# Fused attention and gated MLP: the rows of block 0 taken straight from the score tile, softmax ahead of the conversion in four steps, one score unit fewer in step 0

## The chip, the cores and the metric

The kernel runs on one core of a Trainium2 chip. The core has five engines that matter here: TensorE (PE) with its matrix product and, beside it, the loading of weights (PEld); VectorE (DVE); ScalarE (ACT); GpSimd (POOL); and SyncE (SP), which in this kernel does nothing but issue DMA transfers. Data lies in DRAM, in SBUF (128 partitions, the place of the tiles) and in PSUM (the banks into which PE writes).

The metric is the device time of one execution in microseconds (us), as the median of several runs. A profiled execution has its own time, and in it a span, from the first to the last recorded instruction.

## The reference, cut to what matters

```python
# q, k, v: (8, 12, 448, 64); w_pre, w_post: (12, 12); fp32 throughout
scores = np.matmul(q, k.transpose(0, 1, 3, 2)) / np.sqrt(64)
scores = np.einsum('bhij,hg->bgij', scores, w_pre)         # mix over the heads
scores = scores - np.max(scores, axis=-1, keepdims=True)
attn = np.exp(scores)
attn = attn / (np.sum(attn, axis=-1, keepdims=True) + 1e-09)
attn = np.einsum('bhij,hg->bgij', attn, w_post)            # mix over the heads
out = np.matmul(attn, v)
x = out.transpose(0, 2, 1, 3).reshape(3584, 768)
a, b = x @ w1, x @ w2                                      # (768, 1024) each
y = ((a * b) @ w3) @ w_out                                 # (1024, 1024), (1024, 768)
```

The part of the program that the change touches computes the scores of batch element 0, mixes them over the heads and takes the softmax of the first rows.

## The kernel before, in words

**Rows and blocks.** After the scores come the two mixes over heads. For these the kernel needs a tile in which one partition holds one row of one head. It takes 10 query rows (IB) of 12 heads (H) at a time: 120 partitions (GI) with 448 elements each, a *row block*. A batch element has 45 of them (NB; the last ones overlap or are short), and the main loop runs over all row blocks of all batch elements, one a step.

**From scores to rows.** PE computes the scores of a head for 112 query rows at a time (JT; four such chunks make the 448): partition = query row. A row block wants partition = (query row, head). The turn is made through DRAM: the scores of batch element b are stored to `raw_d[b]`, with the shape [448 rows, 12 heads, 448 columns], and `fetch(n)` (line 217) loads row block n from there into the tile `r`, one transfer of 120 rows of 1,792 bytes. Three buffers hold `r` tiles in turn.

**Batch element 0 at the start.** Queries and keys arrive for two heads (a *pair*, six of them) in the tiles `kqz0` to `kqz5`: a first part (the first 112 query columns and all keys) and a second part (the other query columns, line 867, `others(p)`). `qk_first(p, c, banks)` computes chunk c of pair p; its two matrix products (line 158, tile `psz`) are copied out of PSUM by DVE and, for the second head, by DVE or ACT (lines 163 and 164). For chunk 0 the copies go into one SBUF tile that holds the 112 rows of all 12 heads, `sz`; they are stored to DRAM in two parts. The first FIRST = 48 rows are stored pair by pair (line 168, six stores of 48 rows of 3,584 bytes):

```python
        if c == 0:
            dst, st = dst[:FIRST], st[:FIRST]
        return lambda: nc.sync.dma_start(dst, st)
```

The remaining 64 rows go for all pairs at once, 21,504 bytes a row, when the loads of the first row blocks are already issued (line 800, below the "big store"):

```python
        held = lambda: nc.sync.dma_start(self.raw_d[0][FIRST:JT], self.sz[FIRST:])
```

The other three chunks of the six pairs are 18 *score units*, handed out over the steps 0 to 14 (`firsts`, line 803); one such unit is called ahead of the conversion of the step and any others behind it. A unit needs the second part of its pair's `kqz`.

**A step of the main loop** (`for n in range(N + 6)`) issues, in program order: the load of row block n + 4 (`fetch`), stores that were put off (`do_later`), a second part of `kqz` (`others(n + 3)`), then work on the engines: conversion pieces, `softmax(n)`, `scale(n - 1)`, a split of rows for a later step (`split_r`), score units, the second mix of an earlier block (`post`) and the first mix of the next one, `mix(n + 1)`. The first mix is a product on PE with a block-diagonal `w_pre` (line 235 in the first 20 row blocks, `psm<-r,wsc`). The softmax is a minimum on DVE (`mn`), and the exponential with its running sum on ACT (line 249, `e`, `sm`).

**Conversion.** Beside that, the weights of the MLP arrive as words (`cs`, line 96: `cs3<-wo` is a 128 x 768 piece of w_out's words), go through a square on ACT (line 102, `cm<-cs`), four operations on DVE and a split into a high and a low part (a cast on ACT at line 121, and POOL). `converting()` is a generator, and each `next(...)` makes one piece; the pieces feed `folding`, the product of w3 and w_out.

**What sets the order.** On every engine the instructions run in the order in which the program is written. All DMA transfers go through SP's queue, one behind the other; a store or load that has to wait for data (or for a semaphore of an earlier transfer) holds up those behind it. So the order of SP around the big store is that of these lines:

```python
        others(0)
        others(1)
        for n in range(LF - 1):     # LF = 4
            self.fetch(n)
        next(fold_pieces)
        next(fold_pieces)
        held()
```

Tiles named below: `kqz` (queries and keys of a pair), `psz` and `sz` (scores in PSUM and SBUF), `r` (row block), `wpre_s` and `wsc` (the block-diagonal matrix of the first mix, as loaded and scaled), `psm` (mixed scores), `mn`, `e`, `sm` (minimum, exponential, sum), `cs`, `cm`, `cx`, `fw`, `fo` (conversion and its results).

Of the kernel before, what the change touches and what calls it, by code (L numbers as in the profile page):

```python
# [6 lines left out]
F32 = mybir.dt.float32  # L7
# [8 lines left out]
B, H, S, D = 8, 12, 448, 64  # L16
DM, FF = 768, 1024
HP = H // 2
IB = 10
GI = H * IB  # L20
NB = -(-S // IB)
JT, NJ = 112, 4
# [1 line left out]
NG = NB // GB  # L24
KF, K1 = FF // 128, DM // 128
WHOLE = 20
FIRST = 48
CW = 384
DH = DM // 2
LATE = 2 * NB + GB + 2  # L30
# [15 lines left out]
class Kernel:  # L46
# [102 lines left out]
    def qk_first(self, p, c, banks):  # L149


        nc, t = self.nc, self.kq0s[p]
        cols = slice(c * JT, (c + 1) * JT)
        q = slice(S + cols.start, S + cols.stop) if c else slice(0, JT)
        ps = [self.bank(i, f"psz{p}_{c}_{s}")[:JT, :S] for s, i in enumerate(banks)]
        for s in range(2):
            rows = slice(s * D, (s + 1) * D)
            nc.tensor.matmul(ps[s], t[rows, q], t[rows, JT:JT + S], start=True, stop=True)
        if c == 0:
            st = self.sz[:, 2 * p:2 * p + 2]  # L160
        else:
            st = (self.qp if p % 2 else self.kp).tile([JT, 2, S], F32, tag="st", name=f"sz{p}_{c}", bufs=2)
        nc.scalar.copy(st[:, 0], ps[0])
        (nc.scalar.copy if c else nc.vector.tensor_copy)(st[:, 1], ps[1])
        dst = self.raw_d[0][cols, 2 * p:2 * p + 2, :]
        if c == 0:
            dst, st = dst[:FIRST], st[:FIRST]
        return lambda: nc.sync.dma_start(dst, st)

    def load_kq(self, b, p):  # L170
# [571 lines left out]
    def run(self):  # L742
        nc, tc = self.nc, self.tc
# [29 lines left out]
            nc.sync.dma_start(self.kq0s[p][:, :JT + S], self.kq0[p][:, :JT + S])  # L773
        self.sz = self.mp.tile([JT, NJ, H, GB * IB], F32, tag="mt", name="sz")
        self.sz = self.sz.rearrange("p j g i -> p (j g i)")[:, :H * S].rearrange("p (h j) -> p h j", h=H)
        w = self.kp.tile([128, S], F32R, tag="qh", name="wpre_s").bitcast(F32)[:GI, :GI]
        self.wsc = cp.tile([GI, GI], F32, name="wsc")
        nc.sync.dma_start(w, self.wpre)
# [8 lines left out]
        self.wph = cp.tile([GI, GI], F32R, name="wph")  # L787
        self.wpl = cp.tile([GI, GI], F32R, name="wpl")
        held = []
        for p in range(HP):  # L790
            held.append(self.qk_first(p, 0, ((0, 1), (2, 3), (6, 7))[p % 3]))
            if p > 1:
                held.pop(0)()
        nc.vector.tensor_copy(self.wph, self.wsc)
        nc.vector.tensor_tensor(self.wpl, self.wsc, self.wph.bitcast(F32), op=ALU.subtract)
# [2 lines left out]
        for f in held:  # L798
            f()
        held = lambda: nc.sync.dma_start(self.raw_d[0][FIRST:JT], self.sz[FIRST:])  # L800
        firsts = {}
        for u in range(HP, HP * NJ):
            firsts.setdefault((u - HP) * 15 // (HP * NJ - HP), []).append((u % HP, u // HP))

# [1 line left out]
        for b in range(1, B):  # L808
            first, per, ahead = (12, 26 / 48, 2) if b == 1 else ((b - 1) * NB - 6, 45 / 48, 3)
            for u in range(H * NJ):  # L810
                h, c = divmod(u, NJ)
                n = first + int(u * per)
# [10 lines left out]
        N = B * NB  # L823
# [29 lines left out]
        def advance(count):  # L853
            nonlocal done
            for _ in range(min(count, total - done)):
                next(background)
                done += 1

        def there(p):

            f, r = divmod(p - 3 - 2 * KF, 3)
            return 2 * KF * 3 * (1 + f) + (0, 9, 18)[r] if f >= 0 else min(max(3 * (p - 3), 0), KF * 3)

        wanted, LF, turn = 0, 4, itertools.chain((6, 7, 0) * 9, itertools.cycle((6, 7)))
        self.v_list = [(b, a, g) for b in range(B) for a in range(NG) for g in range(HP)]
        def others(p):
            nc.sync.dma_start(self.kq0s[p][:, JT + S:], self.kq0[p][:, JT + S:])

        others(0)
        others(1)  # L870
        for n in range(LF - 1):
            self.fetch(n)
        next(fold_pieces)
        next(fold_pieces)
# [15 lines left out]
        for n in range(N + 6):  # L890
            self.step = n
            if n == GB + 1:
                self.close("qp")
                self.xp = [self.pool("xp0", 1)]
            if n == SWITCH:
                assert done == total
                next(background, None)
                self.do_ends()
                self.do_soon()
                self.do_later()  # L900
                assert not fold_pieces
                self.close("fp")
                self.wp = self.pool("wp", 5, side="right")
                self.up = self.pool("up", 1, side="right")
                self.xp.append(self.pool("xp1", 1, side="right"))
                background, total, done = self.experts(phases), (E_1 + E_2) * ONE + P_1 * (B - ONE) // 2, 0
            if n == LATE:
                assert done >= E_1
                self.close("xp0", "cx")
                self.xq, self.cb = self.pool("xq", 2), self.pool("cb", 1)  # L910
            if n == PAIR:

                assert done >= 2 * E_1 + E_2 and unit_pieces is None and not self.jobs and not self.ys
                self.do_ends()
                self.do_soon()
                self.do_later()
                self.pairs, self.w_ahead = True, 4
                self.close("xp1", "cb", "xq", "cs")
                self.xq = self.pool("xq", 2)
                self.up2 = self.pool("up2", 1, side="right")  # L920
                self.free += range(N_UP, NS)
                setup = self.pair_setup(phases)
            if PAIR <= n < PAIR + 7:
                next(setup, None)
            if LF <= n + LF < N:
                self.fetch(n + LF)
            self.do_later()
            if n + 3 < HP:
                others(n + 3)
            elif 2 * HP - 3 <= n < 2 * HP:  # L930
                self.load_v()
            for x in loads.get(n, []):
                self.load_kq(*x)
            for x in splits.get(n, []):
                self.split_kq(*x, nc.gpsimd, nc.gpsimd)

            p, pieces = self.n_made - 1 if fold_pieces else 2 * KF + 3 * KF, None
            if avs.get(n):
                pass
            elif fold_pieces:  # L940
                f = (self.n_made - 1 - 2 * KF) // 3
                if f < 2 or done >= 2 * KF * 3 * (f - 1):
                    pieces = fold_pieces
                    if next(pieces, self) is self:
                        fold_pieces = pieces = None
            if n < N:
                self.softmax(n)
            if 0 <= n - 1 < N:
                self.scale(n - 1)
            if n + 2 < N:  # L950
                self.split_r(n + 2)
            self.do_soon()
            for x in firsts.get(n, [])[:1]:
                self.later.append(self.qk_first(*x, (next(turn), next(turn))))
            for x in qks.get(n, []):
                store = self.qk(*x, nq % 2, nc.scalar.copy)
                nq += 1
                if store:
                    self.later.append(store)
            if pieces:  # L960
                next(pieces)
            elif unit_pieces and not fold_pieces and not avs.get(n):
                ahead = 1 if n < SWITCH else 2 * done // (3 * K1) + 4 + (done > 0)
                if n_pieces < ahead:
                    n_pieces += 1
                    if next(unit_pieces, self) is self:
                        unit_pieces = None
                    else:
                        next(unit_pieces)
            now = share.get(n, 0)  # L970
            if n < SWITCH:

                wanted += now
                now = max(min(there(p), KF * 3 + wanted) - done, 0)
            self.do_sums()

            advance(now // 2)
            if 0 <= n - 2 < N:
                self.post(n - 2)
            for x in firsts.get(n, [])[1:]:  # L980
                self.later.append(self.qk_first(*x, (next(turn), next(turn))))
            for x in avs.get(n, []):
                self.av(*x)
            advance(now - now // 2)
            if n + 1 < N:
                self.mix(n + 1)
            self.do_ends()
# [68 lines left out]
```

## Time and profile before

| | |
|---|---|
| Median of 3 runs | 1639.13 us (1638.95 to 1643.07) |
| Profiled execution | 1639.43 us, span 1637.7 us |
| Mean granted clock of PE | 0.993 |
| PE busy | 1579.9 us, 96% of the span |
| PEld, DVE, ACT, POOL busy | 86%, 63%, 61%, 65% of the span |
| DMA | 446.10 MB in 233,906 packets, mean 272 GB/s |

How to read the rows that follow. A group of instructions is given as line, engine, operation and its tiles as out<-in, with the shapes and the count (x). In a timeline the first two columns are start and duration in us from the start of the span, and a bracket tells the idle time ahead of the instruction and what ended it. "SPq" is SP's queue of DMA issues: the duration there is the time that the issue took on the queue, with whatever it waited for, not the transfer. The DMA view gives for each kind of transfer the count, the size and the median time from issue to landing, and for a window the packets by size and their rate. The granted clock of PE is given as a share of full speed. Tile names leave out the buffer number, so `kqz` is any of the six and `r` any row block.

### The profile page before, as it was taken

To read this page: it belongs to the slowest core of one execution; us is meant where nothing else is said; L and a number is where in the kernel's file an instruction comes from. 1 tells how busy PE (TensorE), PEld (TensorE's weight loads), DVE (VectorE), ACT (ScalarE), POOL (GpSimd) and SP (SyncE) were. 2 spreads that over 40 slices of the span, in tenths; PEclk is the share of its full clock that TensorE was granted. 3 is DMA by queue.
4 is the path that set the end of the run, shared out by engine and by line. 5 is a ranking of instruction groups with operands and counts; after the bars stand their busy time and mean duration, and the time that the engine had idled before them with its cause. 6 is when DMAs were issued, how large, how long until landed. Compare 5 with 4: busy or idle time off the path is not lost. (4 is left out here: it accounts for less than half of the span.)

```text
span 1637.7 us, 31687 instructions
## 1 busy us (share of the span) xinstructions
PE 1579.9 (96%) x10528; PEld 1414.0 (86%) x10528; DVE 1030.6 (63%) x2302; ACT 997.3 (61%) x2413; POOL 1068.5 (65%) x902
## 2 busy tenths in 40 slices
PE   5999999999999999999999999999999999999999
PEld 2578997887898888889899898899999898999988
DVE  5967768778747767863465565745555557634573
ACT  4877657677666776776666666666765554542321
POOL 1346546667657788885576776876675666655774
PEclk7999999999999999999999999999999999999999
DMA  8988879898899999999978977889978756678875
GB/s 263 342 269 275 255 223 302 277 310 288 264 279 310 321 341 315 323 335 306 312 240 279 290 243 238 257 270 309 305 248 250 238 188 196 211 229 302 281 233 179
DMA packets 233906, 446.10 MB, mean 272 GB/s; under 512 B 21838, under 2 KB 159054, under 8 KB 233678
## 3 DMA queue, kind: packets, MB, share of 16 engines
q1 hardware_dynamic: 233742, 444.08, 84.6%
q8 instruction: 83, 1.36, 0.4%
q14 instruction: 81, 0.66, 0.1%
HBM read 309.90 MB, written 134.09 MB: 271 GB/s over the span
## 5 line engine op out<-in xcount | busy, mean ns | idle before, releaser
L227 POOL TENSOR_TENSOR rl<-r,rh 120x448 fp32r<-120x448 f32 (+1 forms) x340 | 425.0, 1250 | 321.9 <-DVE rh L226 108.0
L246 DVE TENSOR_REDUCE mn<-psm 120x1 f32<-120x448 f32 x360 | 223.8, 622 | 410.1 <-PE psm L240 395.1
L249 ACT ACTIVATE e<-psm,mn 120x448 f32<-120x448 f32 x360 | 228.5, 635 | 348.1 <-DVE sa L258 293.4
L272 PEld LDWEIGHTS pso<-w,e 120*112 120x112 f32 (+1 forms) x2880 | 345.5, 177 | 49.4 <-ACT mt L278 35.0
L272 PE MATMUL pso<-w,e 120*112 120x120 f32 (+1 forms) x2880 | 358.9, 267 | 20.6 <-ACT mt L278 20.2
L703 PE MATMUL e<-eh,wu 128*128 128x448 f32 x1008 | 304.4, 371 | 1.1 <-DVE c L657 1.1
L278 ACT COPY mt<-pso 112x480 f32<-112x480 f32 x360 | 206.9, 575 | 14.9 <-PE pso L272 9.9
L703 PEld LDWEIGHTS e<-eh,wu 128*128 128x128 f32 x1008 | 187.3, 188 | 16.1 <-DVE c L657 1.9
L226 DVE CAST rh<-r 120x448 fp32r<-120x448 f32 (+1 forms) x340 | 189.9, 559 | 4.1 <-DMA r<-raw_d 3.0
L703 PE MATMUL e<-el,wu 128*128 128x448 f32 x504 | 187.6, 372 | 2.4 <-POOL el L642 2.4
L198 ACT COPY st<-psq 112x448 f32<-112x448 f32 x336 | 173.3, 527 | 25.8 <-DMA raw_d<-st 25.7
L303 PE MATMUL psa<-mt,v 112*64 112x150 f32 (+1 forms) x2304 | 156.9, 292 | 1.9 <-DMA v<-v 1.9
L183 POOL TENSOR_TENSOR ql<-kq,qh 128x448 fp32r<-128x448 f32 x84 | 99.2, 1181 | 85.1 <-ACT qh L181 84.9
L303 PEld LDWEIGHTS psa<-mt,v 112*64 112x64 f32 x2304 | 143.6, 137 | 8.1 <-DMA v<-v 2.3
L657 DVE TENSOR_TENSOR c<-c,e 128x448 f32<-128x448 f32 x168 | 101.2, 615 | 70.4 <-PE e L703 65.8
L193 PE MATMUL psq<-kk,qh 128*112 128x448 f32 x336 | 125.7, 374 | 8.0 <-ACT st L198 7.8
L238 PE MATMUL psm<-rh,wph 120*120 120x448 f32 (+1 forms) x340 | 129.6, 381 | 0.0
L523 PE MATMUL eg<-xh,wu 128*128 128x448 f32 x384 | 127.3, 381 | 0.0
L240 PE MATMUL psm<-rl,wph 120*120 120x448 f32 (+1 forms) x340 | 124.1, 365 | 0.6 <-POOL rl L227 0.5
L239 PE MATMUL psm<-rh,wpl 120*120 120x448 f32 (+1 forms) x340 | 124.2, 365 | 0.0
L194 PE MATMUL psq<-kk,ql 128*112 128x448 f32 x336 | 122.8, 365 | 0.0
L642 POOL TENSOR_TENSOR el<-x,eh 128x448 fp32r<-128x448 f32 x90 | 105.7, 1195 | 9.3 <-DMA x<-x_d 5.3
(114 smaller groups left out, 2961.7 us busy)
## 6 DMA issues: line engine op xcount, KB each, us to landing
r<-raw_d SPq DMA_DIRECT2D x352, 210.0 KB, 4.1
raw_d<-st SPq DMA_DIRECT2D x168, 392.0 KB, 4.7
wu<-w_d SPq DMA_DIRECT2D x104, 384.0 KB, 5.6
wu<-s_d SPq DMA_DIRECT2D x96, 384.0 KB, 4.4
v<-v SPq DMA_DIRECT2D x144, 224.0 KB, 5.1
kq<-kq SPq DMA_DIRECT2D x42, 672.0 KB, 7.0
wu<-w_d SPq DMA_DIRECT2D x51, 512.0 KB, 5.9
wu<-s_d SPq DMA_DIRECT2D x36, 512.0 KB, 4.4
```

Of the source, the lines that this page charges most:

```text
L193: nc.tensor.matmul(p, qh[:, cols], kk, start=True, stop=False)
L198: copy(st[:, c % 2], p)
L226: nc.vector.tensor_copy(rh[:K], r[:K])
L227: nc.gpsimd.tensor_tensor(rl[:K], r[:K], rh[:K].bitcast(F32), op=ALU.subtract)
L238: nc.tensor.matmul(p[:K, :S], self.wph[:K, :K], rh[:K], start=True, stop=False)
L246: nc.vector.tensor_reduce(mn[:K], p[:K, :S], axis=AX.X, op=ALU.min)
L249: nc.scalar.activation(e[:K], p[:K, :S], AF.Exp, bias=mn[:K], scale=-1.0, accum_out=sm[:K])
L272: nc.tensor.matmul(p[:, j, :, :w], e[:K, j * JT:(j + 1) * JT], w2[:K, :, :w], start=True, stop=True)
L278: self.ends.append((4, lambda: copy(dst, p[:, :, :, :w])))
L303: nc.tensor.matmul(self.psa[rows, g % 3, :W], v[:, j, rows], mt[:, j, 2 * g + s, :W], start=(j == 0), stop=(j == NJ - 1))
L523: nc.tensor.matmul(p, u[:, k % (K1 // 2), x], xs[y][:, k], start=(k == 0 and t == 0), stop=(k == K1 - 1 and t == 2))
L703: nc.tensor.matmul(p, w[:, k, x], ops[m, k][y], start=(k == 0 and t == 0), stop=(k == nk - 1 and t == 2))
```

## The change

It has four parts.

1. **Row block 0 from SBUF.** In chunk 0, `qk_first` now copies the first 10 rows of each head straight from the score tile into the tile `r` of row block 0, every twelfth partition of it: 12 copies of 10 rows of 1,792 bytes, those of the even heads issued by ACT and those of the odd heads by SP. The load of row block 0 from DRAM goes. The pairs' row stores leave these 10 rows out. FIRST becomes 50, so a row store has 40 rows instead of 48, and the big store 62 instead of 64. A pair's copies are issued when its scores are computed; its row store is put off for three pairs instead of two.
2. **kqz0's second part** is issued right behind the six first parts, ahead of `wpre`, instead of behind the row stores.
3. **Softmax ahead of the conversion** in the steps 0 to 3.
4. **Score units**: one in step 0 instead of two, and the other 17 spread over the steps from 1 on.

```diff
-FIRST = 48
+FIRST = 5 * IB
...
         if c == 0:
-            dst, st = dst[:FIRST], st[:FIRST]
+
+            for h in range(2 * p, 2 * p + 2):
+                (nc.sync if h % 2 else nc.scalar).dma_start(self.rs[0][h::H], self.sz[:IB, h])
+            dst, st = dst[IB:FIRST], st[IB:FIRST]
         return lambda: nc.sync.dma_start(dst, st)
...
             nc.sync.dma_start(self.kq0s[p][:, :JT + S], self.kq0[p][:, :JT + S])
         self.sz = self.mp.tile([JT, NJ, H, GB * IB], F32, tag="mt", name="sz")
...
+        nc.sync.dma_start(self.kq0s[0][:, JT + S:], self.kq0[0][:, JT + S:])
         w = self.kp.tile([128, S], F32R, tag="qh", name="wpre_s").bitcast(F32)[:GI, :GI]
         self.wsc = cp.tile([GI, GI], F32, name="wsc")
         nc.sync.dma_start(w, self.wpre)
...
         held = []
+        self.rs[0] = self.rp.tile([GI, S], F32, tag="r", name="r0", bufs=3)
         for p in range(HP):
             held.append(self.qk_first(p, 0, ((0, 1), (2, 3), (6, 7))[p % 3]))
-            if p > 1:
+            if p > 2:
                 held.pop(0)()
...
         held = lambda: nc.sync.dma_start(self.raw_d[0][FIRST:JT], self.sz[FIRST:])
         firsts = {}
         for u in range(HP, HP * NJ):
-            firsts.setdefault((u - HP) * 15 // (HP * NJ - HP), []).append((u % HP, u // HP))
+            firsts.setdefault((u - HP - 1) * 14 // (HP * NJ - HP - 1) + 1, []).append((u % HP, u // HP))
...
-        others(0)
         others(1)
-        for n in range(LF - 1):
+        for n in range(1, LF - 1):
             self.fetch(n)
         next(fold_pieces)
         next(fold_pieces)
...
             for x in splits.get(n, []):
                 self.split_kq(*x, nc.gpsimd, nc.gpsimd)
+            if n < 4:
+                self.softmax(n)
 
             p, pieces = self.n_made - 1 if fold_pieces else 2 * KF + 3 * KF, None
...
-            if n < N:
+            if 4 <= n < N:
                 self.softmax(n)
             if 0 <= n - 1 < N:
                 self.scale(n - 1)
```

The order of the instructions on the engines that the change moves, before and after. (The lines of the code shift by three to five, so that the big store is L800 before and L805 after.)

SP (its DMA issues) in the start, from the words `cs1` of w3 on to the second part of pair 1, before. The row stores of line 168 write the first rows of the score tile `sz` to `raw_d`:

```order
L96 DMA cs1_145<-w3t 128x3x256
L168 DMA raw0_d_62<-sz_136 48x896 x4
L96 DMA cs2_192<-w3t 128x2x256
L168 DMA raw0_d_62<-sz_136 48x896 x2
L867 DMA kqz0_124<-kq0 128x336
L867 DMA kqz1_125<-kq0 128x336
```

And after (six of the twelve copies are here, the other six on ACT):

```order
L96 DMA cs1_146<-w3t 128x3x256
L169 DMA r0_151<-sz_136 10x448 x4
L171 DMA raw0_d_62<-sz_136 40x896
L169 DMA r0_151<-sz_136 10x448
L171 DMA raw0_d_62<-sz_136 40x896
L169 DMA r0_151<-sz_136 10x448
L171 DMA raw0_d_62<-sz_136 40x896
L96 DMA cs2_205<-w3t 128x2x256
L171 DMA raw0_d_62<-sz_136 40x896 x3
L872 DMA kqz1_125<-kq0 128x336
```

The copies into `r0` come ahead of and between the row stores, which move behind them, and kqz0's second part has left this place.

SP right behind that, around the big store, before:

```order
L217 DMA r0_206<-raw0_d_62 120x448
L217 DMA r1_208<-raw0_d_62 120x448
L217 DMA r2_210<-raw0_d_62 120x448
L96 DMA cs3_212<-wo 128x768
L800 DMA raw0_d_62<-sz_136 64x5376
L96 DMA cs4_226<-wo 128x768
L217 DMA r3_240<-raw0_d_62 120x448
L867 DMA kqz2_126<-kq0 128x336
L217 DMA r4_243<-raw0_d_62 120x448
```

And after:

```order
L220 DMA r1_219<-raw0_d_62 120x448
L220 DMA r2_221<-raw0_d_62 120x448
L96 DMA cs3_223<-wo 128x768
L805 DMA raw0_d_62<-sz_136 62x5376
L96 DMA cs4_237<-wo 128x768
L220 DMA r3_251<-raw0_d_62 120x448
L872 DMA kqz2_126<-kq0 128x336
L220 DMA r4_254<-raw0_d_62 120x448
```

The load of r0 is gone, the big store has 62 rows, and what stands ahead of and behind it is otherwise the same: kqz2 is the third transfer behind it.

PE from the first mix on (row block 0), before:

```order
L235 MATMUL psm0_238<-r0_206,wsc_138 120x448
L158 MATMUL psz0_1_0_257<-kqz0_124 112x448
L158 MATMUL psz0_1_1_258<-kqz0_124 112x448
L158 MATMUL psz1_1_0_270<-kqz1_125 112x448
L158 MATMUL psz1_1_1_271<-kqz1_125 112x448
L235 MATMUL psm1_277<-r1_208,wsc_138 120x448
L158 MATMUL psz2_1_0_301<-kqz2_126 112x448
L158 MATMUL psz2_1_1_302<-kqz2_126 112x448
L235 MATMUL psm2_314<-r2_210,wsc_138 120x448
```

And after:

```order
L238 MATMUL psm0_249<-r0_151,wsc_139 120x448
L158 MATMUL psz0_1_0_268<-kqz0_124 112x448
L158 MATMUL psz0_1_1_269<-kqz0_124 112x448
L238 MATMUL psm1_281<-r1_219,wsc_139 120x448
L158 MATMUL psz1_1_0_304<-kqz1_125 112x448
L158 MATMUL psz1_1_1_305<-kqz1_125 112x448
L158 MATMUL psz2_1_0_317<-kqz2_126 112x448
L158 MATMUL psz2_1_1_318<-kqz2_126 112x448
L238 MATMUL psm2_324<-r2_221,wsc_139 120x448
```

The mix of row block 1 moves ahead of the score unit of pair 1; the unit of pair 2, which needs kqz2, keeps its place ahead of the mix of block 2.

ACT in the first two steps, before:

```order
L121 CAST fw0_214<-cx2_236 128x2x128
L102 ACTIVATE cm3_250<-cs3_212 128x384
L249 ACTIVATE e0_254,sm0_255<-psm0_238,mn0_252 120x448
L163 COPY sz0_1_261<-psz0_1_0_257 112x448
L164 COPY sz0_1_261<-psz0_1_1_258 112x448
L163 COPY sz1_1_274<-psz1_1_0_270 112x448
L164 COPY sz1_1_274<-psz1_1_1_271 112x448
```

And after:

```order
L252 ACTIVATE e0_259,sm0_260<-psm0_249,mn0_257 120x448
L121 CAST fw0_225<-cx2_247 128x2x128
L102 ACTIVATE cm3_266<-cs3_223 128x384
L163 COPY sz0_1_272<-psz0_1_0_268 112x448
L164 COPY sz0_1_272<-psz0_1_1_269 112x448
L252 ACTIVATE e1_289,sm1_290<-psm1_281,mn1_287 120x448
L121 CAST fo_143<-cx3_279 128x384
L102 ACTIVATE cm4_296<-cs4_237 128x384
L163 COPY sz1_1_308<-psz1_1_0_304 112x448
```

The exponential of block 0 moves ahead of the cast and of the square that wants cs3, and pair 1's copy out of PSUM moves behind the exponential of block 1 and the square that wants cs4. On DVE and POOL the order is the same before and after.

## The prediction

> **What bounds the kernel now.** I read the page first (parts 1 and 2), then the busy times by stage, cut where the picture of TensorE (PE) changes (after each engine's busy time its instructions; the last three columns are the granted clock, the DMA engines' busy share and what they moved), then PE's own timeline in the start, and from its last wait back to SyncE's (SP's) transfers.
>
> ```profile
> core 0: us, PE busy (x) PEld busy (x) DVE busy (x) ACT busy (x) POOL busy (x), PEclk, DMA share, GB/s
> 20.00:32.00 12.00, 6.97 (x14) 2.10 (x14) 5.57 (x12) 4.79 (x12) 1.72 (x2) 0.64 0.89 264
> 32.00:38.00 6.00, 6.00 (x16) 2.06 (x17) 2.97 (x9) 3.23 (x8) 1.00 (x1) 0.57 0.94 303
> 38.00:64.00 26.00, 25.82 (x131) 15.03 (x130) 23.33 (x52) 20.11 (x48) 6.02 (x6) 1.00 0.99 338
> 64.00:100.00 36.00, 30.81 (x136) 17.55 (x136) 28.54 (x69) 31.06 (x76) 17.16 (x16) 0.91 0.97 332
> 100.00:1637.60 1537.60, 1502.11 (x10218) 1373.67 (x10214) 960.01 (x2143) 931.22 (x2262) 1040.41 (x871) 1.00 0.85 270
> ```
>
> From 100 us on PE is busy 1502.1 of 1537.6 us at full clock, and from 38 to 64 us 25.8 of 26. What the change moves lies ahead of that. So whatever it does to the moment at which PE runs without a stop goes into the end almost one to one; only the stage from 64 to 100 us, in which PE stands 5.2 us, could take some of it up.
>
> PE's timeline of the start (start, duration, line, tiles; in brackets the idle time before and what ended it):
>
> ```profile
> 20.18 1.82 PE L235 MATMUL psm<-r,wsc 120*120 120x448 f32 x2 [8.21 <-DMA r<-raw_d]
> 21.93 2.54 PE L158 MATMUL psz<-kqz 64*112 64x448 f32 x6
> 25.78 1.00 PE L158 MATMUL psz<-kqz 64*112 64x448 f32 x2 [1.31 <-ACT sz L163]
> 26.71 1.64 PE L235 MATMUL psm<-r,wsc 120*120 120x448 f32 x2
> 31.89 1.84 PE L158 MATMUL psz<-kqz 64*112 64x448 f32 x4 [3.54 <-DMA kqz<-kq]
> 33.66 1.85 PE L235 MATMUL psm<-r,wsc 120*120 120x448 f32 x2
> 35.44 1.84 PE L158 MATMUL psz<-kqz 64*112 64x448 f32 x4
> ```
>
> The change is aimed at the first wait, 8.21 us for the rows r0. But the last wait decides: at 31.89 PE has stood 3.54 us for the second part of pair 2's queries (kqz2, line 867), and from there on it runs. Everything ahead of 31.89 may move by some us and PE still waits for kqz2. So I follow kqz2. SP's timeline; below it the time from issue to landing (last column) of single transfers, from the DMA view of windows around one issue: the issues at 19.15 and 18.75, then those at 19.85 and 22.68, and r0's at 17.39:
>
> ```profile
> 17.39 1.25 SPq L217 DMA_DIRECT2D r<-raw_d  x3
> 18.75 0.36 SPq L96 DMA_DIRECT2D cs<-wo  x1
> 19.15 0.61 SPq L800 DMA_DIRECT2D raw_d<-sz  x1
> 19.85 0.53 SPq L96 DMA_DIRECT2D cs<-wo  x1
> 20.43 2.21 SPq L217 DMA_DIRECT2D r<-raw_d  x1
> 22.68 2.52 SPq L867 DMA_DIRECT2D kqz<-kq  x1
> 29.31 0.35 SPq L217 DMA_DIRECT2D r<-raw_d  x1
> ```
>
> ```profile
> raw_d<-sz SPq DMA_DIRECT2D x1, 1344.0 KB, 10.1
> cs<-wo SPq DMA_DIRECT2D x1, 384.0 KB, 5.3
> ...
> cs<-wo SPq DMA_DIRECT2D x1, 384.0 KB, 10.5
> ...
> kqz<-kq SPq DMA_DIRECT2D x1, 168.0 KB, 9.1
> ...
> r<-raw_d SPq DMA_DIRECT2D x1, 210.0 KB, 2.6
> ```
>
> The big store of line 800 (the rest of the score tile, 64 rows of 21,504 bytes) is issued at 19.15 and lands 10.1 us later, at 29.25. cs4 and kqz2, issued behind it, land behind it, at 30.3 and 31.8, though a transfer of kqz2's size is soon done: r0, which is larger, took 2.6 us in an emptier queue. So kqz2 is late because it stands behind the big store, and the question is what the change does to that store: its FIRST goes from 48 to 50, and the store from 64 rows to 62.
>
> **How many DMA engines a transfer uses.** The small packets tell: the DMA queue over the whole span, then from 19.0 to 19.5 us, then in two windows of 0.02 us (packets, MB, share of 16 engines).
>
> ```profile
> DMA packets 233906, 446.10 MB, mean 272 GB/s; under 512 B 21838, under 2 KB 159054, under 8 KB 233678
> ...
> r<-raw_d SPq DMA_DIRECT2D x352, 210.0 KB, 4.1
> ...
> wpre_s<-wpre SPq DMA_DIRECT2D x1, 56.2 KB, 4.7
> ```
>
> ```profile
> DMA packets 112, 0.17 MB, mean 348 GB/s; under 512 B 15, under 2 KB 112, under 8 KB 112
> ```
>
> ```profile
> q1 hardware_dynamic: 1, 0.02, 249.7%
> ...
> q1 hardware_dynamic: 1, 0.02, 533.1%
> ```
>
> The whole list of issues adds up to 1372 transfers. Of the 21,838 packets under 512 bytes, 240 are the rows of wpre and of wpo, its like (120 of 480 bytes each). 21,598 remain. With one closing packet from each of 16 engines they would be 21,952; 354 are missing, exactly as many as there are transfers of 120 rows (352 + 2). So a transfer of 120 rows runs on 15 engines, 8 rows each, and those of 128, 112, 96, 64 and 48 rows on 16. The second fence shows it once: from 19.0 to 19.5 us, when r0 finishes, 15 small packets. Rows dealt out one by one would have used 16 engines for 120 rows; groups of eight would have used 6 for 48. Two readings are left. (A) Equal shares: the largest number up to 16 that divides the rows. (B) Rows over 16, rounded up, for each engine until none is left. They agree on every count of this trace and part at 62: by A 2 engines with 31 rows, by B 16 with up to 4. I take A, since no transfer in the trace has an unequal share. The Trainium skill's page "DMA: Bandwidth & Descriptors" (section "Why a DMA increments its semaphore by 16 and not by 1") says that a transfer issued on SP or ACT takes the largest k up to 16 that divides the slowest dimension of both sides. By that rule the sum is the one below, by B about 1639; the trace agrees with it at 120 rows, and no run here shows 62.
>
> The price of a row: in each of the two short windows, at 23.68 and 22.82 us, one packet of the big store starts. 2.497 x 16 x 0.02 = 0.80 us; the other took 1.71 us. I take 0.80, which is 27 GB/s; the stage from 38 to 64 us moved 338/16 = 21 GB/s per engine, beside many others, so 1.02 us is the slow end.
>
> **The change part by part.**
> - The big store, by A: 31 x 0.80 = 24.8 us. When does it start? Ahead of it SP now issues six copies into r0 (the other six go from ACT), and one load less. At 1.25/3 = 0.42 us each that is at most +2.1 us, and at least 0 if SP's waits for landings hide them; I take +1.0, so 20.2. r0's 2.6 us less 0.5 for its data make 2 us from issue to the first packet, and r1, r2, cs3 ahead of it about 0.5: start 22.7, end 47.5. Ends: 22.2 and, if it waits for all of cs3 (18.75 + 5.3 + 1), 25.1.
> - kqz2 behind it: today 31.8 - 29.25 = 2.5 us later. It keeps its share on each engine, the store's two among them, so it lands at 50.0 instead of 31.8: **+18.2 us**. PE stands in that time. Late next are cs4 and r3, which land just ahead of kqz2.
> - r4 no longer waits for the store's landing (SP stands today from 25.2 to 29.3): 0, for it lands behind the store anyway. r5 still waits for it.
> - r0 straight from the score tile: mix(0) some 3 us earlier, at best; cost or gain 0 while kqz2 decides. The six issues on ACT, at 0.42 each, lie ahead of 20 us where PE stands: 0, at most 2.5 us, which also lies ahead of 31.89. Row stores of 40 rows: by A 10 engines with 4 rows instead of 16 with 3: 0 for the same reason.
> - kqz0's second part ahead of wpre: 168 KB at the 264 to 338 GB/s of the stages delay wpre and wsc by 0.5 to 0.7 us. PE needs wsc at 20 us only: 0.
> - Softmax ahead of the conversion: today ACT's exp of row block 0 stands behind the square that waits for cs3:
>
> ```profile
> 24.14 0.55 ACT L102 ACTIVATE cm<-cs 128x384 f32<-128x384 f32 x1 [3.91 <-DMA cs<-wo]
> 24.60 0.61 ACT L249 ACTIVATE e<-psm,mn 120x448 f32<-120x448 f32 x1
> ```
>
>   Now it stands ahead of it, up to 3.9 us earlier, inside PE's wait: 0. In return pair 1's score copies come behind the square of cs4, which lands just before kqz2, and pair 2 needs a bank that they free: 0 to +0.9 us. I take 0.
> - One score unit in step 0: 1.84 us of PE move behind mix(1), both ahead of 31.89: 0.
>
> Sum: the profiled execution took 1639.43 us (span 1637.7), 0.3 over the median of the runs, 1639.13. On the median: 1639.1 + 18.2 = **1657.3 us**. Ends: start 22.2 gives +17.7; start 25.1 at 1.02 us a row gives 25.1 + 31.6 + 2.5 = 59.2, +27.4. Two unknowns reach below: the stage from 64 to 100 us may give back some of its 5.2 us, and the clock (0.57 to 0.64 here) may come back sooner or later by a us or two. So the likeliest case has 1651 to 1666.
>
> **The rivals.**
> - B, not slower: 62 rows still spread over 16 engines. Then kqz2 moves with SP's order alone: 0 to +2.1 us for the issues, less some 0.6 us for 205 KB that need not be moved (a load of 210 KB, 168 KB of row stores and 42 of the big store go, 215 KB of copies come, at 330 GB/s): -0.6 to +1.5 us, and a step of the clock either way. 1636.5 to 1642, most likely 1639. It decides where the store's landing stays within 12 us of its issue. For it speaks that the store has always been fast; against it the missing packets, which show that the count of rows matters.
> - C, worse: on its two engines each row takes the 1.71 us of the other row shown. 53.0 us, kqz2 at 78: +46, 1685. Against it: long packets mostly lie where several transfers are in flight on one engine.
> - That the change does not do what it says: r0 is complete only after its last copy, which stands behind row stores on SP; mix(0) might start no earlier than 20 us. Under A and B alike that changes nothing at 31.89, so it has no time of its own.
>
> **How the numbers follow.** A 0.86, B 0.10, C 0.04. The prediction is A's 1657.3. For 8 in 10 I take 1649 to 1666, nearly all of A; the rest is B, C and A's edges. 0.3% is 4.9 us, about what a measurement of this kernel can tell from no change. All of A and C is slower by more: 0.90. B is within it but for a small part: same 0.09, faster 0.01.
>
> **What would show it.** After: the big store lands some 27 us after its issue, not 10; a wait of PE for kqz2 of over 20 us that ends near 50; ten small packets, not 16, for each copy into r0 and each row store; DMA share near 2/16 in between, and from 52 us on the old picture, shifted. mix(0) earlier than 20 us. Wrong, if the store lands within 12 us: then it is B, and the time is that of today.

## The result and the profile after

The changed kernel takes 1669.11 us (median of 4 runs, 1668.45 to 1669.17) against 1639.04 us: 1.0179 times as long, 95% interval 1.016 to 1.0197 (here and below the ratio is estimated from the runs of both kernels and isn't the quotient of the two medians; they differ by up to 0.2%). By the medians that is 30.1 us more, where 18.2 were forecast; the range ended at 1666. The direction and the main mechanism were right, the size was not. The profiled execution took 1669.17 us, its span is 1667.4 us.

The busy times by stage, with each stage from 62 us on laid 30 us behind its like of before:

```profile
core 0: us, PE busy (x) PEld busy (x) DVE busy (x) ACT busy (x) POOL busy (x), PEclk, DMA share, GB/s
20.00:32.00 12.00, 6.66 (x10) 1.36 (x6) 5.85 (x14) 3.83 (x10) 1.72 (x2) 0.64 0.75 233
32.00:62.00 30.00, 0.00 (x0) 0.00 (x0) 0.04 (x1) 0.56 (x3) 0.99 (x1) 0.50 0.13 42
62.00:94.00 32.00, 30.85 (x135) 16.16 (x136) 26.65 (x59) 23.78 (x56) 7.04 (x7) 0.89 0.95 304
94.00:130.00 36.00, 30.45 (x130) 17.47 (x129) 28.20 (x66) 30.64 (x73) 16.84 (x16) 0.91 1.00 332
130.00:1667.40 1537.40, 1505.71 (x10231) 1376.65 (x10230) 963.50 (x2148) 931.21 (x2264) 1039.89 (x872) 1.00 0.85 271
```

Everything that was added is the second row: 30 us in which the engines do next to nothing (ACT 0.56 us, POOL 0.99) and the DMA engines are busy for a share of 0.13, which is 2 of 16. From 130 us on the rows are those of before from 100 us on (PE 1505.7 busy us of 1537.4, against 1502.1 of 1537.6 before). PE's timeline names both ends of the hole, SP's what stands in it:

```profile
17.77 1.82 PE L238 MATMUL psm<-r,wsc 120*120 120x448 f32 x2 [3.34 <-DMA r<-sz]
...
25.82 1.85 PE L238 MATMUL psm<-r,wsc 120*120 120x448 f32 x2 [4.60 <-DMA r<-raw_d]
27.60 3.66 PE L158 MATMUL psz<-kqz 64*112 64x448 f32 x4
62.98 1.89 PE L158 MATMUL psz<-kqz 64*112 64x448 f32 x4 [31.71 <-ACT sz L163]
```

```profile
14.20 0.74 SPq L169 DMA_DIRECT2D r<-sz  x1
...
17.44 1.17 SPq L171 DMA_DIRECT2D raw_d<-sz  x3
18.66 0.70 SPq L872 DMA_DIRECT2D kqz<-kq  x1
23.04 0.77 SPq L220 DMA_DIRECT2D r<-raw_d  x2
24.31 0.28 SPq L805 DMA_DIRECT2D raw_d<-sz  x1
24.69 0.36 SPq L96 DMA_DIRECT2D cs<-wo  x1
...
60.84 0.34 SPq L220 DMA_DIRECT2D r<-raw_d  x1
```

The hole begins at about 31.3, where the matmuls of 27.60 end. The first mix starts at 17.77 instead of 20.18 us: the rows of block 0 do come earlier. But the last row stores are issued up to 18.6 us instead of 14.2, r1 and r2 wait on SP until they have landed (23.04), and the big store of 62 rows goes out at 24.31 instead of 19.15. It lands at about 60.8, when SP may issue r5, which needs its rows. cs4 and kqz2, issued behind it, land behind it.

PE's bracket names ACT (pair 1's copy out of PSUM, line 163; lines 163 and 164 are ACT's, but for the second head of a pair in chunk 0, which is DVE's), because that copy now stands behind the square that wants cs4:

```profile
62.01 0.55 ACT L102 ACTIVATE cm<-cs 128x384 f32<-128x384 f32 x1 [29.46 <-DMA cs<-wo]
62.46 0.52 ACT L163 COPY sz<-psz 112x448 f32<-112x448 f32 x1
```

ACT itself waited 29.46 us for cs4. This is the same transfer jam seen one step later, and the order on ACT adds at most a microsecond to it.

The number of engines can be counted again. In the whole span:

```profile
DMA packets 233911, 445.89 MB, mean 267 GB/s; under 512 B 21893, under 2 KB 159109, under 8 KB 233685
```

There are 1383 transfers now. 16 closing packets each would be 22,128. Take off one for each of 353 transfers of 120 rows, 6 for each of the 12 copies (10 rows) and the 6 row stores (40 rows), and 14 for the big store, if it runs on 2 engines: 21,653 remain. With the 240 rows of wpre and wpo that is 21,893, the number counted. ACT's queue shows it for its six copies alone:

```profile
q10 hardware_dynamic: 120, 0.11, 0.0%
```

That is 60 rows and 60 more packets, 10 for each copy of 10 rows.

How fast did the two engines go? Two windows in the hole, at first and then later (packets, MB, rate):

```profile
DMA packets 18, 0.39 MB, mean 55 GB/s; under 512 B 0, under 2 KB 0, under 8 KB 0
```

```profile
DMA packets 26, 0.56 MB, mean 33 GB/s; under 512 B 0, under 2 KB 0, under 8 KB 0
```

From 33 to 40 us 18 rows start, 7 x 2 / 18 = 0.78 us of an engine a row, as forecast. From 41 to 58 us it is 17 x 2 / 26 = 1.31 us, though nothing else is in flight (the windows hold no smaller packets).

### The profile page after: what moved, and what is told of

The parts are those of the page before. It is cut to its first block, busy times and chain, and to the rows that moved or that the text cites. A ratio compares the mean times of both kernels' runs of the same rounds, so it can differ in the third digit from the quotient of the medians.

```text
span 1667.4 us, 31715 instructions
## 1 busy us (share of the span) xinstructions
PE 1585.2 (95%) x10528; PEld 1416.3 (85%) x10528; DVE 1032.4 (62%) x2302; ACT 996.0 (60%) x2413; POOL 1067.7 (64%) x902
## 2 busy tenths in 40 slices
DMA packets 233911, 445.89 MB, mean 267 GB/s; under 512 B 21893, under 2 KB 159109, under 8 KB 233685
```

## The experiments

Each is compared with runs of the kernel before on the same chip, so its ratio counts, not the difference to 1639.04. The time of a single profiled execution can lie some us off the median of its kernel. "Before" and "changed" below are the two kernels.

**1. The changed kernel with its big store in 48 + 14 rows.**

```diff
-held = lambda: nc.sync.dma_start(self.raw_d[0][FIRST:JT], self.sz[FIRST:])
+def held():
+    nc.sync.dma_start(self.raw_d[0][FIRST:98], self.sz[FIRST:98])
+    nc.sync.dma_start(self.raw_d[0][98:JT], self.sz[98:])
```

> The changed kernel with its big store cut in two, rows 50 to 97 (48 rows) and rows 98 to 111 (14 rows). Theory 1 (the number of rows sets the number of engines: 62 = 2 x 31 gives 2, 48 gives 16, 14 gives 14): the store is done some 10 us after its issue again. Its issue stays at 24.3 us instead of 19.15, so PE's last wait of the start ends near 37 instead of 31.9 and the time is +5 us or less over before: 1640 to 1645 us. Theory 2 (it is the first partition, 50 instead of 48, that makes the store slow): the 48 rows still begin at partition 50, so the time stays near 1669. Theory 3 (it is the copies into r0 and the late row stores that cost): also near 1669.

Measured 1644.71 us against 1637.67, ratio 1.0031 (1.0017 to 1.0045). PE's last wait ends at 38.04:

```profile
38.04 1.84 PE L158 MATMUL psz<-kqz 64*112 64x448 f32 x4 [7.27 <-ACT sz L163]
```

The same rows from the same partitions, cut in two, take some 24 us off 1669.1. Theories 2 and 3 fall as explanations of the bulk; some 5 us remain.

**2. The kernel before with its big store in 62 + 2 rows** (the same edit with the cut at 110).

> The kernel before, all of it, but its big store of 64 rows cut into 62 rows (48 to 109) and 2 rows. Theory 1: 62 rows run on 2 engines; issued at 19.15, first row at 21.7, 31 rows an engine at the 1.05 us a row that the changed kernel's trace averages gives a landing near 55 and kqz2 near 57.5 instead of 31.8: +25 us, 1664 (at 0.80 us a row, 1657). Theory 2 (first partition) and theory 3 (copies and late row stores): nothing of theirs is in it, 1639.

Measured 1663.64 us against 1637.67, ratio 1.0145 (1.0126 to 1.0165). PE's wait and SP's issue of the row block that needs the store:

```profile
57.76 1.84 PE L158 MATMUL psz<-kqz 64*112 64x448 f32 x4 [30.04 <-DMA kqz<-kq]
```

```profile
19.72 0.28 SPq L801 DMA_DIRECT2D raw_d<-sz  x1
...
53.61 0.32 SPq L217 DMA_DIRECT2D r<-raw_d  x1
```

Two rows fewer in one transfer (they go as a store of their own), and nothing else of the change, cost 26 us. Here PE's bracket names kqz2, as the prediction had it.

**3. The kernel before with its big store in 61 + 3 rows** (the cut at 109).

> The kernel before with its big store cut into 61 rows (48 to 108) and 3 rows. Theory 1: 61 is prime, so one engine takes all rows: 61 x 0.80 to 1.10 us = 49 to 67 us after 21.7, landing at 71 to 89, time 1679 to 1697 us. If instead anything not a multiple of 16 falls back to two engines: as with 62 rows, 1657 to 1664. If the rows are dealt out, 1639.

Measured 1681.36 us against 1637.67, ratio 1.0248 (1.0229 to 1.0268). The store is issued at 19.11 and lands at 72.1. The window from 40 to 70 us:

```profile
DMA packets 37, 0.80 MB, mean 27 GB/s; under 512 B 0, under 2 KB 0, under 8 KB 0
q1 hardware_dynamic: 37, 0.80, 6.2%
```

6.2% is one engine of 16. It needs 30 / 37 = 0.81 us a row, and it doesn't slow down. So fewer rows take longer: the divisor of their number counts, not the amount.

**4. The changed kernel with the stores of before**: FIRST is 48 again and a row store has all 48 rows.

```diff
-FIRST = 5 * IB
+FIRST = 48
-            dst, st = dst[IB:FIRST], st[IB:FIRST]
+            dst, st = dst[:FIRST], st[:FIRST]
```

> The changed kernel with FIRST at 48 and row stores of all 48 rows (the 10 rows that r0 has got directly are stored too), so both kinds of stores have the sizes of before, and the rest of the change stays. Theory 1: the big store takes 10 us again; issued 3 to 5 us later than before because the row stores are, the time is 1639 to 1644. Theory 3: stays near 1669. The difference to the run with 48 + 14 rows shows what row stores of 40 instead of 48 rows cost (10 engines with 4 rows each, against 16 with 3): 0 to 2 us.

Measured 1643.26 us against 1637.67, ratio 1.0028 (1.0015 to 1.0041). SP issues the big store at 24.26, and PE's last wait ends at 36.84:

```profile
24.26 0.59 SPq L805 DMA_DIRECT2D raw_d<-sz  x1
```

```profile
36.84 1.84 PE L158 MATMUL psz<-kqz 64*112 64x448 f32 x4 [5.18 <-ACT sz L164]
```

Row stores of 40 instead of 48 rows make no difference that the intervals of runs 1 and 4 would show (the two also differ in the big store, 48 + 14 rows against 64). What remains of the change still costs 0.3%, and its PE starts 5 us late.

**5. The kernel before with its big store in 16 + 34 + 14 rows**, to see why two engines slow down.

> The kernel before with its big store cut into 16, 34 and 14 rows (48 to 63, 64 to 97, 98 to 111); 34 = 2 x 17, so the middle piece runs on 2 engines by the count of rows. It is to tell why the rows of the 2-engine stores took 0.80 us each at first and 1.3 us later. Theory H (where the two engines read): the slow part begins when both read partitions from 64 on; here both do so from the first row (64 to 80 and 81 to 97), so rows take about 1.3 us from the start, some 22 us for 17. Theory G (a matter of how far the transfer has come, or of the partitions from 96 on): 17 rows at 0.80 us, some 13.6 us, with two slow ones at most. Time: the store lands 15 to 24 us after its first row instead of 7: 1643 to 1655 us.

One run, 1650.02 us. From about 30 to 36.6 us nearly all rows of the 34-row store take 0.80 us on both engines. Only its last three, the 17th of one engine and the 16th and 17th of the other, take 1.2 to 1.4 us, and the row of the next store behind them on each of these engines 1.95 and 0.91. Theory H falls: if the shares are consecutive rows, both engines read from partition 64 on all the time.

**6. The kernel before with the rest of the change, without the copies**: kqz0 early, softmax ahead, one score unit in step 0; r0 comes from DRAM and the stores are those of before. The edits are the parts 2 to 4 of the change.

> The kernel before with everything of the change but the copies into r0, their held-back row stores and FIRST: kqz0's second part ahead of wpre, softmax ahead of the conversion in steps 0 to 3, one score unit in step 0. Theory C (the 5 us that the changed kernel loses even with stores on 16 engines come from the copies, whose issues on ACT and SP make the row stores and with them r1 and the big store late): the big store is issued near 19 us again, PE's last wait ends near 32, time 1636 to 1640 us. Rival D (they come from the early load or the new order on ACT and PE): PE's last wait ends near 37 and the time is 1641 to 1645 us.

Measured 1637.45 us against 1638.84, ratio 0.9985 (0.9974 to 0.9996).

```profile
20.40 0.61 SPq L801 DMA_DIRECT2D raw_d<-sz  x1
```

```profile
32.32 1.84 PE L158 MATMUL psz<-kqz 64*112 64x448 f32 x4 [3.81 <-DMA kqz<-kq]
```

Without the copies the loss is gone, as theory C of the expectation has it; these three parts may even gain a little. This is the only version whose interval lies below the kernel before. The big store still goes out at 20.40 instead of 19.15, so not all of its delay is the copies'.

**7. Run 4 with the row stores held back for two pairs** (`p > 1`).

> The changed kernel with stores of 48 and 64 rows as in the run before (FIRST 48, whole row stores), and a pair's row store held back for two pairs instead of three, as in the kernel before. If holding them back is what makes the big store late, its issue goes from 24.3 back to 20 to 21 us and the time to 1638 to 1640 us. If the copies' own issues do (0.73 us each on ACT, between the copies of the scores out of PSUM, and as much on SP), it stays at 23 to 25 us and the time at 1641 to 1645 us.

Measured 1644.18 us against 1638.84, ratio 1.0023 (1.001 to 1.0037). SP's timeline:

```profile
16.44 0.74 SPq L169 DMA_DIRECT2D r<-sz  x1
17.28 0.41 SPq L171 DMA_DIRECT2D raw_d<-sz  x1
18.26 1.36 SPq L171 DMA_DIRECT2D raw_d<-sz  x2
...
24.14 0.59 SPq L805 DMA_DIRECT2D raw_d<-sz  x1
```

The hold is not it: the big store goes out at 24.14. This execution took 1639.46 us, no more than the profiled one of before, though PE's last wait ended at 36.11 instead of 31.89. A late start of some 4 us can be lost in what one execution does later, so for these few us the interval counts and not the trace's own time.

**8. The kernel before with its big store in two of 32 rows**, the second behind kqz3.

```diff
+held = lambda: nc.sync.dma_start(self.raw_d[0][FIRST:80], self.sz[FIRST:80])
+held2 = lambda: nc.sync.dma_start(self.raw_d[0][80:JT], self.sz[80:])
...
                 others(n + 3)
+                if n == 0:
+                    held2()
```

> The kernel before with its big store cut into two of 32 rows (48 to 79, 80 to 111; 16 engines each), the second issued in step 0 behind kqz3's second part. It carries the reading that PE's wait of 3.54 us at 28.35 is that for kqz2 behind the big store. With half of the store ahead of it kqz2 lands near 27 to 28 us, the wait goes, and PE runs from 28 us on or waits up to 1 us for the next rows: 1635.5 to 1638 us against some 1639. Rival: the transfers all pass through the same 16 engines, 0.89 to 0.99 busy from 20 to 64 us, so what comes early here is missing later (in the stage from 64 to 100 us), and the time stays within 1 us of before.

Measured 1638.18 us against 1638.84, ratio 0.9992 (0.9981 to 1.0003): the same. PE's waits:

```profile
26.65 1.83 PE L158 MATMUL psz<-kqz 64*112 64x448 f32 x2 [0.92 <-ACT sz L163]
38.48 1.42 PE L158 MATMUL psz<-kqz 64*112 64x448 f32 x4 [2.20 <-ACT fo L121]
```

The wait of 3.5 us for kqz2 is gone, which shows that the big store made it; 2.2 us come back at 36 us behind ACT's conversion. The rest of the gain is too small to measure.

**9. Two added stores of 34 rows**, one that writes raw0's rows 78 to 111 from partitions 0 to 33, one that reads partitions 78 to 111 and writes raw7; the big store itself goes in two of 32 rows.

> The kernel before with two more stores of 34 rows (2 engines by the count) ahead of its big store, which is cut into two of 32 rows: first the score tile's partitions 0 to 33 to the rows 78 to 111 of raw0 (written over afterwards), then its partitions 78 to 111 to the rows 0 to 33 of raw7 (likewise). The rows of 2-engine stores took 0.80 us each until one of the engines came to row 95 to 98, and 1.3 us on the average from there; these are partitions and rows of raw0 with the same number. If it is the partition that is read (from about 96 on): the first store takes 17 x 0.80 = 13.6 us, the second about 17 x 1.3 = 22 us. If it is the place that is written in DRAM: the first has its last two or three rows slow, the second none. If it is how far a transfer has come: both alike. The time is only that of two added transfers: 1665 to 1680 us.

One run, 1666.72 us. The window from 27 to 33 us, in the first store:

```profile
DMA packets 15, 0.32 MB, mean 54 GB/s; under 512 B 0, under 2 KB 0, under 8 KB 0
```

6 x 2 / 15 = 0.80 us a row; it took 13.5 us for its 17 rows an engine. The second took 13.9 us on one engine and 15.8 on the other, far from 22. So neither the partition nor the place in DRAM slows the rows by itself. Nor does the progress of a transfer alone explain it: run 5's rows slowed at the 16th or 17th of 17, the first store's here not at all.

What both runs leave untested is the pair of partitions that the two engines read at one time. If an engine's share is consecutive rows, the two read 31 partitions apart in the changed kernel and in run 2, and 17 apart in runs 5 and 9. In the slow stretches of these two kernels 0.80 us comes back with every fourth row: the rows of partitions 72 and 103, and of 76 and 107, took 0.80 to 0.82 us on both engines in both, while rows between took up to 1.9. Run 5's last rows don't fit a pattern of pairs as simple as this.

**10. Run 7 with all twelve copies on ACT.**

> The kernel of the run before with stores of 48 and 64 rows and a hold of two pairs, but all twelve copies into r0 issued by ACT and none by SP. There the scores are copied out of PSUM by 13.9 us with and without the copies, and SP issues its last row store at 19.2 us with them and at 15.3 without. If SP's own issues of six copies (0.74 us each, each behind data and landings) make the row stores and the big store late, the big store's issue comes from 24.1 back to 21 to 22.5 us (ACT issues three copies more by the time of the last scores, 2.2 us), and the time is 1638 to 1642 us. If it is the copies as transfers, or their place ahead of the row stores in the data's order, the issue stays at 24 us and the time at 1641 to 1645 us.

Measured 1642.44 us against 1638.86, ratio 1.0023 (1.0013 to 1.0033). The big store goes out at 23.63, later than I expected, because ACT's last copy of scores out of PSUM comes late:

```profile
17.62 1.55 ACTq L169 DMA_DIRECT2D r<-sz  x2
19.21 0.53 ACT L163 COPY sz<-psz 112x448 f32<-112x448 f32 x1 [1.62 <-DMA r<-sz]
```

At 19.2 us instead of 13.3, as in runs 6 and 7: what SP is spared, ACT pays.

**11. Run 6 with the two halves of run 8.**

> The kernel before with what of the change cost nothing (kqz0's second part early, softmax ahead of the conversion, one score unit in step 0) and its big store cut into two of 32 rows, the second behind kqz3. PE's wait for kqz2 (3.8 us with the first three alone) should go or shrink below 1 us. If nothing takes it back later, 1634 to 1636 us; if the stage from 64 to 100 us takes it back, as the run with the two halves alone suggests (a new wait of 2.2 us at 36 us, and 1638.2), 1636.5 to 1638.5 us.

Measured 1637.46 us against 1638.86, ratio 0.9993 (0.9982 to 1.0005): no more than either part.

```profile
29.92 2.63 PE L158 MATMUL psz<-kqz 64*112 64x448 f32 x4 [1.95 <-ACT fo L121]
```

Again a wait for a bank behind ACT's conversion stands where the one for kqz2 stood.

**12. Run 7 with all twelve copies on POOL.**

> The kernel of the run with stores of 48 and 64 rows and a hold of two pairs, but all twelve copies into r0 issued by POOL, which has nothing else to do before 12 us. With six of them on SP and with all on ACT the big store was issued at 24.1 and 23.6 us: on SP they stand between the row stores, on ACT between the copies of the scores. Theory Q (the copies cost by the time of their issue on a queue that something else needs): now neither queue has them, so the last row store is issued near 15.5 us, the big store near 20.5, PE's last wait ends near 32 and the time is 1636 to 1639.5 us; r0 may come later than with SP and ACT if POOL takes over 1 us for an issue. Theory T (they cost as transfers, ahead of the row stores on the DMA engines): the big store stays near 24 us and the time at 1641 to 1645 us.

Measured 1641.58 us against 1637.61, ratio 1.0028 (1.0019 to 1.0037). POOL issued nine copies in 4.67 us from 10.36 on; on SP:

```profile
15.49 2.21 SPq L171 DMA_DIRECT2D raw_d<-sz  x2
17.75 1.25 SPq L872 DMA_DIRECT2D kqz<-kq  x1
21.80 0.78 SPq L220 DMA_DIRECT2D r<-raw_d  x2
22.67 0.36 SPq L96 DMA_DIRECT2D cs<-wo  x1
23.09 0.61 SPq L805 DMA_DIRECT2D raw_d<-sz  x1
```

Theory Q falls. Neither SP nor ACT issues a copy, yet the last row stores are out only at 17.7 and the big store at 23.1. The copies cost 2.7 to 3.9 us of its start on whichever queue they are issued (runs 4, 7, 10 and 12: 23.1 to 24.3); without them (run 6) it is 20.4. The first mix, which the copies were to bring forward, starts at 22.35 here, later than the 20.18 of before. In what way they hold up the others from POOL was not separated.

## Why the prediction was right in kind and wrong in size

- **How many engines a transfer uses.** Reading A held, and B is out: 62 rows on 2 engines (runs 1 and 2, and the count of packets), 61 on 1 (run 3). The Trainium skill's page "DMA: Bandwidth & Descriptors" (section "Why a DMA increments its semaphore by 16 and not by 1") gives that rule, the largest number up to 16 that divides the slowest dimension; the traces agree, 2 for 62 rows and 1 for 61. C, two engines at 1.71 us a row, is out as well, but the mean of 1.06 us a row lies between A's 0.80 and C's price.
- **kqz2 behind the big store.** Right: PE's last wait of the start moved from 31.89 to 62.98, 31.1 us, and the span grew by 29.7. That ACT's order would cost 0 to 0.9 us on top was right too: the square and the copy behind cs4 took 62.01 to 62.98.
- **The price of a row** is the step that failed most. Of the two rows that I had seen I took the cheaper, 0.80 us, for all 31. It holds for the first 16; the 31 took from 27.65 to 60.44, 32.8 us or 1.06 each, instead of 24.8: 8.0 us of the miss. My slow end, 1.02, was the better figure, though for other reasons: not other transfers slow the rows, they are gone by then. On a single engine each row takes 0.80 us (run 3).
- **The start of the store** is the other mis-sized term. I took the six issues on SP at 0.42 us each, "at most +2.1", and +1.0 for the sum. The store was issued at 24.31, not 20.2 (4.1 us), and its first row came 3.3 us later, not 2.5 (0.8 us). A copy's issue takes 0.74 us, and the row stores behind them, for which r1 waits, go out 4.4 us later. The copies cause most of it, as run 6 (20.40) against runs 4 and 7 (24.26 and 24.14) shows. I had priced their issues on the two queues; a moved step also counts with what waits for the landing of what it displaces.
- **kqz0's second part ahead of wpre** was put at nothing because PE needs wsc only at 20 us. That reason was wrong: DVE makes wsc from wpre, and DVE's copies of the scores out of PSUM, for which the row stores wait, stand behind that instruction. Before and after:

```profile
8.24 0.22 DVE L786 TENSOR_SCALAR wsc<-wpre_s 120x120 f32<-120x120 f32 x1 [8.24 <-DMA wpre_s<-wpre]
```

```profile
9.43 0.22 DVE L790 TENSOR_SCALAR wsc<-wpre_s 120x120 f32<-120x120 f32 x1 [9.43 <-DMA wpre_s<-wpre]
```

  With this load early and no copies (runs 6 and 11) the big store went out at 20.40 and 20.10; with neither, at 19.15 in the kernel before and at 19.11 to 19.87 in runs 2, 3 and 8. So some 0.2 to 1.3 us of the 5.2 by which the store is late are probably this load's; no run has it alone.
- 8.0 + 4.1 + 0.8 = 12.9 us, and PE's restart missed its forecast of 50.0 by 13.0. I had allowed for the stage behind the hole to give back up to 5.2; it gave back nothing. The mix that starts at 112.02 before starts at 143.78 after, 31.8 us later. The span grew by 29.7, so some 2 us came back after that: PE is busy 193.1 us from 600 to 800 before, and 196.2 from 630 to 830 after. The change does not touch that stage, so what came back there is luck and not the give-back that I had in mind.
- **r0 straight from the score tile** gained 2.4 us at mix(0), which the prediction expected to vanish in the next wait; they did. Softmax ahead, kqz0 early and the score unit were put at nothing: together 0.15% in their favour in run 6, with an interval from 0.04 to 0.26%.
- **The range** went wrong by its slow end: start 25.1 with 1.02 us a row. The first row came at 27.65. A bound made from the issue's length alone is not a bound if data and landings stand ahead of it as well.

## What to carry to other kernels

Before you change the number of rows of a transfer, look at its divisors: on this chip 64 rows ran on 16 engines, 62 on 2 and 61 on 1, and a transfer on few engines holds back what is queued behind it (PE's wait behind it ended at 62.98 us instead of 31.89). If the number has no large divisor up to 16, cut the transfer, as into 48 + 14. And count what a small added transfer displaces: twelve copies of 17.5 KB brought one mix forward by 2.4 us and made the store that PE ends up waiting for 2.7 to 3.9 us later.

## What was not expected of the hardware

- Two engines alone slowed from 0.80 us a row (54 GB/s together) to 1.31 (33 GB/s) half-way through a store, at about 40.4 us in the changed kernel and 38.3 in run 2; one engine alone did not (27 GB/s in run 3). Runs 5 and 9 speak against the partition, the place in DRAM and the progress of the transfer, each as a cause by itself. The pair of partitions read at one time is untested, and the cause stays open.
- The issue of a copy of 10 rows from SBUF to SBUF took 0.74 us on SP and ACT, while that of a load of 120 rows took 0.42 before; on POOL a copy took 0.52.
